# Chunk bounds on eight array tiles at once, some transposes by DMA, and a written-out order, in a chunk-selecting attention with a phase mixer

## The chip, the cores and the metric

The kernel runs on one core of a Trainium2 chip. The metric is the device time of one execution, in microseconds (us). TensorE (PE) multiplies; VectorE (DVE) and ScalarE (ACT) move results out of PSUM, the memory that PE writes; GpSimd (POOL) converts types and masks; SyncE (SP) issues every DMA, in order. Each engine works through its own queue in order.

## The reference

```python
# q, k, v: (4 batches, 8 heads, 768 positions, 64), fp32; chunks of 32 positions, so 24 chunks
ub = np.sum(np.maximum(q * k_min, q * k_max), axis=-1)     # bound of each query on each chunk (k_min, k_max: per chunk)
ub = np.where(causal, ub, -1e9)
top_chunks = np.argsort(ub, axis=-1)[..., -6:]             # six chunks for each query
scores = np.where(sel & causal_pos, q @ k.T / 8, -1e9)
x = softmax(scores) @ v                                     # heads side by side: (4, 768, 512)
theta = x @ w_theta
zr, zi = x * np.cos(theta), x * np.sin(theta)
y = w_tok_r @ zr + w_tok_i @ zi                             # over the 768 positions
u = x + y
out = u + np.maximum(u @ w_ch, 0)
```

## The kernel before

A batch has two groups of four heads. For a group, `keys` reduces k to the chunks' maxima and minima (three DVE steps for each) and writes them, with signs, to `bnd`. `queries` turns q on PE (fp32, into `psq`) and splits it by sign into two `ubq` tiles of two heads each, 64 rows of the 128 for a head. `choice` multiplies `bnd` and `ubq` in fp32 on PE (tile `psub`, L517), copies the result to `ubm`, turns it on PE (`psut`, L532), adds the causal mask (`ubs`, L537), finds the sixth largest of 24 with DVE's MAX8 (`top`, L547) and compares (L558); the result goes into `qe`, next to q, and a DMA transpose gives `qext`. It does all this in two parts, of two and of three blocks of 128 queries (`PARTS`); queries 0 to 127 need no choice. An fp32 matmul shows as two weight loads and two MATMUL records, one for each of its two passes. In L517 a matmul takes 128 rows (two heads) and 64 columns of the array, so that one part has four: two halves of the sum by two pairs of heads, the pairs on columns 0 to 63 and 64 to 127.

`attend` makes the scores of a head (`psc`, L622), the exponential (ACT, `pt`, L631), the mask on the diagonal (POOL, L642), and the product with v (`psav`, L653); DVE normalises into `x` (L669). When a batch is done, `transpose16` turns x into `xT` in four pieces `c` of two heads each (six fp16 PE transposes L688 and one copy L693 for a piece), `phases` makes theta (`pst`, L708), cosine and sine (ACT, L716) and `zz` (DVE, L722), and `mixer` the token products (`psy`, in the last batch also `psz`, L749 and L751), u (DVE, L761), its transpose `uT` and the last product (`pso`, L784, `ot`, L789). In batches 1 and 2 a DMA transpose turns u (`UDMA`); in batches 0 and 3 PE does, with four transposes (L772) and a copy for each block of 128 positions. The phases and the mixer of a batch are woven into the next batch's attention; those of batch 3 stand alone at the end.

All work is handed to `Plan` as some 1450 tasks. `Plan.order` plays them through with estimated durations, keys and a table of shifts (`SHIFT`), and gives the order in which they are written; tasks that ACT or DVE can do go to one of them there. PSUM is given out as two double banks `sc` (scores, and `psz`), one `av`, and three banks `mi` for all else. 34 `fill` matmuls (L899) keep PE going at the start.

Of the kernel before, what the change touches and what calls it, by code (L numbers as in the profile page):

```python
# [9 lines left out]
FP32 = mybir.dt.float32  # L10
# [6 lines left out]
class Task:  # L17
    __slots__ = ("i", "eng", "dur", "fn", "key", "deps", "succ", "alloc", "uses", "opts", "lock", "psum",
                 "after_start", "left", "ready", "start", "end", "kind", "group", "bias")


class Plan:
# [9 lines left out]

    LAT = {"PE": 0.22, "ACT": 0.08, "DVE": 0.08, "POOL": 0.08, "SP": 2.0}

    def __init__(self, bufs, in_order, hot, boost, shift):
        self.tasks = []
        self.bufs = bufs
        self.in_order = in_order
        self.count = {}
        self.hot, self.boost = hot, boost  # L40
        self.shift, self.group = shift, None
        self.turn = {}
        self.writers, self.readers = {}, {}
        self.tag_of, self.users = {}, {}

    def add(self, eng, dur, key, fn, r=(), w=(), new=(), after=(), kind=None, lock=False):
        t = Task()
        t.i, t.eng, t.dur, t.fn, t.key, t.kind = len(self.tasks), eng, dur, fn, key, kind
        t.opts = eng if isinstance(eng, dict) else {eng: dur}
        t.lock = lock or eng == "POOL"  # L50
        t.key += self.shift.get(self.group, 0.0)
        t.group = self.group
        t.bias = self.shift.get(("dve", self.group), 0.0)
        t.deps, t.after_start, t.succ, t.alloc, t.uses = set(), set(), [], [], []
        for name, tag in new:
            self.tag_of[name] = tag
            self.turn[name] = self.count.get(tag, 0)
            self.count[tag] = self.turn[name] + 1
            self.users[name] = []
            t.alloc.append(name)  # L60
        names = [n for n, _ in new]
        t.psum = [n[0] for n in r if isinstance(n, tuple) and self.tag_of.get(n[0]) in self.hot]
        if isinstance(eng, dict) or eng in ("ACT", "DVE"):
            if t.psum:
                t.key -= self.boost
        else:
            t.psum = []
        for n in list(r) + list(w) + names:
            base = n[0] if isinstance(n, tuple) and n and n[0] in self.users else n
            if base in self.users and t not in self.users[base]:  # L70
                self.users[base].append(t)
                t.after_start.add(self.users[base][0].i)
                t.uses.append(base)
# [3 lines left out]
        for n in list(w):  # L77
            t.deps |= set(self.readers.get(n, ()))
            t.deps |= set(self.writers.get(n, ()))
            self.writers[n] = [t.i]  # L80
            self.readers[n] = []
        for n in names:
            self.writers[n] = [t.i]
        t.deps |= set(a.i for a in after)
        t.deps.discard(t.i)
        t.after_start -= t.deps | {t.i}
        self.tasks.append(t)
        return t

    def order(self):  # L90
        T = self.tasks
        for t in T:
            t.left = len(t.deps) + len(t.after_start)
            t.ready = 0.0
            t.start = None
            for d in t.deps:
                T[d].succ.append(t.i)
            for d in t.after_start:
                T[d].succ.append(t.i)
        placed = {}  # L100
        pending = {}
        freed, last = {}, {}
        for n, us in self.users.items():
            pending[n] = len(us)
        free_at = dict.fromkeys(("PE", "ACT", "DVE", "POOL", "SP"), 0.0)
        mode = [None]
        cand = {e: [] for e in free_at}
        for t in T:
            if t.left == 0:
                for e in t.opts:  # L110
                    cand[e].append(t)
        reader, port = {}, 0.0
        n_done, seq = 0, []
        now = 0.0

        def begin(t, e):
            s = max(free_at[e], now, t.ready, port if t.lock else 0.0)
            for n in t.psum:
                if n in reader and reader[n][0] != e:
                    s = max(s, reader[n][1] + 0.1)  # L120
            return s

        while n_done < len(T):
            best = None
            for e, c in cand.items():
                at = max(free_at[e], now)
                pick = None
                for t in c:
                    s = begin(t, e)
                    ok = True  # L130
                    if len(t.opts) > 1:
                        mine = s + t.opts[e] + (t.bias if e == "DVE" else 0.0)
                        for o, d in t.opts.items():
                            if o != e and begin(t, o) + d + (t.bias if o == "DVE" else 0.0) < mine:
                                ok = False
                    own = {}
                    for n in t.alloc:
                        tag = self.tag_of[n]
                        ring = placed.setdefault(tag, [])
                        m = len(ring) + own.get(tag, 0)  # L140
                        own[tag] = own.get(tag, 0) + 1
                        if tag in self.in_order and self.turn[n] != m:
                            ok = False
                            break
                        k = m - self.bufs[tag]
                        if k >= 0:
                            f = freed.get(ring[k])
                            if f is None:
                                ok = False
                                break  # L150
                            s = max(s, f)
                    if not ok:
                        continue
                    if pick is None or (max(s, at + 1e-9), t.key, t.i) < pick[0]:
                        pick = ((max(s, at + 1e-9), t.key, t.i), s, t)
                if pick and (best is None or pick[1] < best[1]):
                    best = pick + (e,)
            assert best is not None, "no task can start"
            _, s, t, _ = best
            for e in t.opts:  # L160
                cand[e].remove(t)
            t.eng = best[3]
            d = t.opts[t.eng]
            if t.kind is not None:
                if mode[0] not in (None, t.kind):
                    d += 1.3
                mode[0] = t.kind
            t.start, t.end = s, s + d
            now = s
            free_at[t.eng] = t.end  # L170
            if t.lock:
                port = t.end
            for n in t.psum:
                reader[n] = (t.eng, max(t.end, reader.get(n, (0, 0.0))[1]))
            lat = self.LAT[t.eng]
            for n in t.alloc:
                placed[self.tag_of[n]].append(n)
            for n in t.uses:
                pending[n] -= 1
                last[n] = max(last.get(n, 0.0), t.end + lat)  # L180
                if pending[n] == 0:
                    freed[n] = last[n]
            for i in t.succ:
                u = T[i]
                u.left -= 1
                same = t.eng != "SP" and list(u.opts) == [t.eng]
                u.ready = max(u.ready, t.start if t.i in u.after_start else t.end + (0.0 if same else lat))
                if u.left == 0:
                    for e in u.opts:
                        cand[e].append(u)  # L190
            seq.append(t)
            n_done += 1
        return seq

    def emit(self):
        for t in self.order():
            t.fn(t.eng) if len(t.opts) > 1 else t.fn()
# [3 lines left out]
def kernel(  # L201
# [19 lines left out]
    NM = 5  # L221
    scale = float(1.0 / np.sqrt(D))
# [17 lines left out]
    qt = P + np.arange(NM)[None, :, None] * P + np.arange(P)[:, None, None]  # L240
    cm_np = np.where(qt // CH >= np.arange(NCH)[None, None, :], 0.0, -1e9).astype(np.float32)
    cm_h = nc.inline_tensor(cm_np.reshape(P, NM * NCH), name="cmask32")
# [5 lines left out]
    cmask32 = const.tile([P, NM, NCH], FP32, name="cmask32", tag="c_cm")  # L248
# [103 lines left out]
    def act_t(n):  # L352
        return 0.19 + n / 1200.0
# [602 lines left out]
```

## Time and profile before

| | us |
|---|---|
| three runs: median (lowest to highest) | 272.23 (272.11 to 273.69) |
| the profiled execution, its own time | 271.77 |
| its span, first to last instruction | 270.0 |
| PE busy, of the span | 240.8 |
| DVE, ACT, POOL busy | 195.5, 162.0, 135.0 |

A row of a group view names line, engine, operation, tiles and shapes, then the busy time of the group, the mean of one in ns, and the idle time before them. A matmul's record lasts longer than the stretch that it keeps the array, since records overlap; the pace is read from starts.

### The profile page before, as it was taken

Reading aid. Unit: us, or ns where it says so; the run is one execution under the profiler, and the core shown is the slowest. Engines: PE = TensorE matmul, PEld = TensorE weight load, DVE = VectorE, ACT = ScalarE, POOL = GpSimd, SP = SyncE. Lnnn points to the kernel's source line nnn. Section 1 sums busy time; section 2 is a strip of 40 time slices with the busy share of each in tenths; the row PEclk is TensorE's granted clock in tenths of the full one; section 3 lists DMA queues with packets and bytes.
Section 4 is the critical chain, followed back from the end, with each engine's and each line's share of the span. In section 5 each row is a group of like instructions: output and inputs, shape, how many; then the busy total and the mean of one; then the engine's idle time right before and its main releaser. Section 6 shows DMA issues by size and latency. Waiting matters only on the chain.

```text
span 270.0 us, 5519 instructions
## 1 busy us (share of the span) xinstructions
PE 240.8 (89%) x2055; PEld 147.8 (55%) x2055; DVE 195.5 (72%) x474; ACT 162.0 (60%) x225; POOL 135.0 (50%) x188
## 2 busy tenths in 40 slices
PE   4896586978689989989999999999999999899993
PEld 1553355666434676655763477666654667434441
DVE  3959689899799594799999985997853436344453
ACT  2349647489559499271938879635687777374000
POOL 7534657668368886968642278536302555100000
PEclk9999598999869999999999999999999999999999
DMA  7897857799989789898988642337180014310123
GB/s 198 199 240 156 213 123 113 199 259 243 252 220 258 191 232 210 185 242 211 257 204 203 121 98 62 70 89 177 22 197 0 19 41 94 141 58 0 41 78 117
DMA packets 90434, 40.71 MB, mean 151 GB/s; under 512 B 83736, under 2 KB 83864, under 8 KB 89736
## 3 DMA queue, kind: packets, MB, share of 16 engines
q1 hardware_dynamic: 90408, 40.37, 61.5%
q8 instruction: 16, 0.26, 0.4%
q14 instruction: 10, 0.08, 0.1%
HBM read 26.20 MB, written 6.29 MB: 120 GB/s over the span
## 4 chain that ended last, share of the span: by engine, by line
PE 56%; DMA 16%; DVE 13%; POOL 8%; issue 3%; SPq 2%; ACT 1%; POOLq 0%; DVEq 0%; ACTq 0%
PE psy L749 8%; PE psy L751 8%; PE psc L622 8%; PE pso L784 6%; PE psub L517 5%; PE psav L653 5%; DMA w<-in_moe_w_tok_r_dram 4%; POOL pt L642 4%; DMA out_dram<-ot 4%; PE pst L708 4%; DMA q<-in_q_dram 3%; DMA w<-in_moe_w_tok_i_dram 3%; PE psq L485 2%; POOL a L809 2%; DVE h L411 2%
## 5 line engine op out<-in xcount | busy, mean ns | idle before, releaser
L631 ACT ACTIVATE pt<-psc 128x1024 f16<-128x1024 f32 (+1 forms) x96 | 83.8, 920 | 37.5 <-PE psc L622 36.4
L642 POOL TENSOR_TENSOR pt<-pt,tri 128x256 f16<-128x256 f16 x96 | 68.3, 722 | 56.8 <-ACT pt L631 55.6
L622 PE MATMUL psc<-qext,kext 88*128 88x512 f16 (+3 forms) x256 | 51.7, 317 | 2.4 <-ACT pt L631 1.6
L749 PE MATMUL psy<-zz,wtokT 128*128 128x512 f16 x120 | 45.5, 379 | 0.9 <-DVE ot L789 0.9
L751 PE MATMUL psy<-zz,wtokT 128*128 128x512 f16 x120 | 45.4, 379 | 0.0
L622 PEld LDWEIGHTS <-kext 88*128 88x128 f16 x256 | 33.8, 153 | 13.6 <-issue 4.1
L653 PE MATMUL psav<-v,pt 128*128 128x65 f16 x672 | 28.0, 194 | 2.2 <-POOL mm L429 2.1
L653 PEld LDWEIGHTS <-pt 128*128 128x128 f16 x672 | 25.3, 98 | 7.9 <-POOL pt L642 2.9
L708 PE MATMUL pst<-wtheta,xT 128*128 128x512 f16 x96 | 25.8, 410 | 1.2 <-ACT xT L693 0.5
L761 DVE TENSOR_TENSOR u<-psy,x 128x512 f16<-128x512 f32 x20 | 13.6, 688 | 16.3 <-PE psy L751 16.3
L411 DVE TENSOR_TENSOR h<-kc 96x1024 f32<-96x1024 f32 (+1 forms) x16 | 21.2, 1327 | 5.3 <-DMA kc<-in_k_dram 5.2
L789 DVE SCALAR_TENSOR_TENSOR ot<-pso,u 128x512 f32<-128x512 f32 x24 | 16.4, 688 | 11.7 <-PE pso L784 8.8
L784 PE MATMUL pso<-wch,uT 128*128 128x512 f16 x96 | 23.5, 379 | 0.6 <-DMA uT<-u 0.6
L751 PEld LDWEIGHTS <-wtokT 128*128 128x128 f16 x144 | 14.1, 98 | 15.9 <-issue 2.3
L493 ACT ACTIVATE ubq<-psq,signs 128x256 f32<-128x256 f32 (+1 forms) x30 | 14.0, 531 | 13.6 <-PE psq L485 13.5
L749 PEld LDWEIGHTS <-wtokT 128*128 128x128 f16 x144 | 14.1, 98 | 14.1
L722 DVE TENSOR_TENSOR zz<-x,cs 128x1024 f16<-128x1024 f16 x24 | 17.7, 755 | 4.8 <-ACT cs L716 4.6
L716 ACT ACTIVATE cs<-pst,pi 128x512 f16<-128x512 f32 x24 | 16.6, 693 | 7.2 <-DVE zz L722 4.9
L517 PE MATMUL psub<-ubq,bnd 128*64 128x384 f32 (+1 forms) x128 | 20.8, 463 | 0.1
L447 POOL CAST ke<-kc 96x1024 f16<-96x1024 f32 x16 | 17.4, 1097 | 6.4 <-DMA kc<-in_k_dram 6.2
L485 PE MATMUL psq<-ident,q 128*128 128x128 f32 x80 | 14.7, 310 | 5.7 <-DMA q<-in_q_dram 3.0
L475 POOL CAST qe<-q 128x768 f16<-128x768 f32 x16 | 16.1, 1010 | 6.1 <-DMA q<-in_q_dram 3.2
(69 smaller groups left out, 364.0 us busy)
## 6 DMA issues: line engine op xcount, KB each, us to landing
q<-in_q_dram SPq DMA_DIRECT2D x32, 192.0 KB, 3.6
v<-in_v_dram SPq DMA_DIRECT2D x64, 96.0 KB, 3.1
out_dram<-ot SPq DMA_DIRECT2D x24, 256.0 KB, 2.3
kc<-in_k_dram SPq DMA_DIRECT2D x7, 768.0 KB, 6.2
w<-in_moe_w_tok_r_dram SPq DMA_DIRECT2D x6, 384.0 KB, 4.7
w<-in_moe_w_tok_i_dram SPq DMA_DIRECT2D x6, 384.0 KB, 4.3
w<-in_moe_w_theta_dram SPq DMA_DIRECT2D x4, 256.0 KB, 2.7
w<-in_moe_w_ch_dram SPq DMA_DIRECT2D x4, 256.0 KB, 3.7
```

The source lines that it names most:

```text
L411: nc.vector.tensor_tensor(out=st[hn].rearrange("p (z w) d -> p z (w d)", z=2)[:, s], in0=kv[:, s, 0], in1=kv[:, s, 1], op=op)
L485: nc.tensor.transpose(t[:, o * P:(o + 1) * P], st[q32][:, n, :, :].rearrange("p x d -> p (x d)"), ident32)
L517: nc.tensor.matmul(t[64 * z:64 * z + 64, :], bnd[g][:, y, 2 * z:2 * z + 2, :].rearrange("p x c -> p (x c)"), st[u][:, y, c0:c0 + w], start ...
L622: nc.tensor.matmul(t[:, a0:a1], kx[0:KX, hj:CH * 96:NCH], qx[0:KX, q0 + a0 - o:q0 + a1 - o], start=True, stop=True)
L631: nc.scalar.activation(out=t[:, BASE[s]:BASE[s] + wa + wb], in_=st[psc][:, 0:wa + wb], func=AF.Exp, bias=0.0, scale=scale)
L642: nc.gpsimd.tensor_tensor(out=d, in0=d, in1=tri16.unsqueeze(1).broadcast_to([P, 2, P]), op=ALU.mult)
L653: nc.tensor.matmul(t[:, a, :], st[pt][:, o:o + P], v16s[g][:, x, j, :], start=(j == 0), stop=(j == a))
L708: nc.tensor.matmul(p, st[xT][:, c, t * P:(t + 1) * P], wtheta16[:, c, :], start=(c == 0), stop=(c == 3))
L722: nc.vector.tensor_tensor(out=st[zz][:, t, :, :], in1=st[cs], op=ALU.mult, in0=st[xx][:, t, :].unsqueeze(1).broadcast_to([P, 2, dm]))
L749: nc.tensor.matmul(acc(), wtokT16[:, i, 0, t * P:(t + 1) * P], st[zz][:, i, 0, :], start=(i == 0), stop=False)
L751: nc.tensor.matmul(acc(), wtokT16[:, i, 1, t * P:(t + 1) * P], st[zz][:, i, 1, :], start=False, stop=(i == NT - 1))
L784: nc.tensor.matmul(p, st[uT][:, c, :], wch16[:, c, :], start=(c == 0), stop=(c == 3))
```

## The change

Four things change.

The bounds: `choice` works on 576 queries (192 to 767) in one go, as two windows of 320 columns that start at 0 and 256 (`th`). A matmul takes one head (64 rows) and 32 columns: two heads `x` by two pairs `z` by two windows are eight positions in the array, each with two halves `y` of the sum, so 16 matmuls stand in a row. The two heads write two PSUM banks of `mi`, taken together. Then, for each bank, come one copy of 320 columns, three transposes (six in place of five for a group), one mask of 288 elements, ten MAX8, and two compares in place of one.

The transposes: pieces 0 to 2 of x are turned by DMA in batches 2 and 3 (`XDMA`), and u of blocks 0 to 3 in batch 3 (`UDMA`). x is kept with a piece's 768 x 128 values together, which changes the strides of the DVE reads of x in L722 and L761 and of the write in L669.

The order: `Plan.order`, its keys and `SHIFT` are gone; a table of numbers, `ORDER`, names the tasks in the order in which they are written, and the sign says DVE or ACT. A path for turning the token weights by DMA exists, but its set is empty.

```diff
-    UDMA = (1, 2)
+    UDMA = {(b, t) for b in (1, 2) for t in range(NT)} | {(3, t) for t in range(4)}
+    XDMA = {(b, c) for b in (2, 3) for c in range(3)}
-        for t in self.order():
-            t.fn(t.eng) if len(t.opts) > 1 else t.fn()
+        for o in self.order:
+            t = self.tasks[~o if o < 0 else o]
...
+    ORDER = (
+        0, 2, 17, 15, 1, 3, 4, 19, 5, 6, 20, 187, 8, 114, 11, 21, 22, 7, 23, 24, 13, 16, 25, 26, 27, 62, 65, 67,
...
-                for y in range(2):
-                    for z, u in enumerate(us):
-                        nc.tensor.matmul(t[64 * z:64 * z + 64, :],
-                                         bnd[g][:, y, 2 * z:2 * z + 2, :].rearrange("p x c -> p (x c)"),
-                                         st[u][:, y, c0:c0 + w], start=(y == 0), stop=(y == 1))
+            ts = [newp(n, "mi", [P, QW], FP32) for n in psub]
+            for y in range(2):
+                for th in range(2):
+                    for z, u in enumerate(us):
+                        for x in range(2):
+                            r = slice(x * D, (x + 1) * D)
+                            c = 32 * (2 * th + z)
+                            nc.tensor.matmul(ts[x][c:c + 32, :], bnd[g][r, y, 2 * z + x, :],
+                                             st[u][r, y, th * 2 * P:th * 2 * P + QW], start=(y == 0), stop=(y == 1))
...
+        if (dst[1], c) in XDMA:
+            def turn():
+                t = new(dst) if c == 0 else st[dst]
+                nc.sync.dma_start_transpose(out=t[:, c, :].rearrange("p (n t) -> p n t", t=P),
+                                            in_=st[src][:, c].rearrange("p n d -> p (n d)"))
...
-            if b in UDMA:
+            if (b, t) in UDMA:
```

Where the instructions stand now, at three places. On PE, the second group of batch 3: the end of its bounds before, where the second part stands 40 rows behind the first,

```order
L653 LDWEIGHTS pt
L653 MATMUL psav<-v_1_75,pt 128x65
L517 MATMUL psub<-ubq,bnd_77 64x384 x4
L532 MATMUL psut<-ident_58,ubm 128x128 x2
L688 LDWEIGHTS x_2149
L688 MATMUL psT<-ident_59,x_2149 128x128
```

and after:

```order
L558 LDWEIGHTS pt
L558 MATMUL psav<-v_1_75,pt 128x65
L421 MATMUL psub<-ubq,bnd_78 32x320 x16
L527 LDWEIGHTS kext_68
L527 MATMUL psc<-qext_70,kext_68 128x512
L527 LDWEIGHTS kext_68
L527 MATMUL psc<-qext_70,kext_68 128x256
```

The two parts have become one burst of 16 matmuls, a piece of the next scores stands behind it, and the turns of x that stood there are gone.

On DVE, the choice of the first group of batch 3. Before:

```order
L537 TENSOR_TENSOR ubs<-psut,cmask_62 128x192
L547 MAX top_2692<-ubs 128x8 x8
L558 TENSOR_TENSOR qe<-ubs,top_2692 128x2x4x24
L537 TENSOR_TENSOR ubs<-psut,cmask_62 128x288
L547 MAX top_2692<-ubs 128x8 x12
L558 TENSOR_TENSOR qe<-ubs,top_2692 128x3x4x24
```

After:

```order
L440 TENSOR_TENSOR ubs<-psut,cmask_62 128x288
L450 MAX top_2705<-ubs 128x8 x10
L463 TENSOR_TENSOR qe<-ubs,top_2705 128x2x3x24
L463 TENSOR_TENSOR qe<-ubs,top_2705 128x2x2x24
L450 MAX top_2705<-ubs 128x8 x10
L705 SCALAR_TENSOR_TENSOR ot<-pso,u_2306 128x512
L463 TENSOR_TENSOR qe<-ubs,top_2705 128x2x3x24
L463 TENSOR_TENSOR qe<-ubs,top_2705 128x2x2x24
```

A mask, a MAX8 row and a compare for each part have become, for each bank, a mask (the first one stands five rows ahead of this piece), a MAX8 row and two compares.

On SP, the last DMAs of the program, from the first turn of u in batch 2 on. Before:

```order
L766 DMA_TRANSPOSE uT_3159<-u_3061 128x4x128
L793 DMA out_dram<-ot 128x512
L766 DMA_TRANSPOSE uT_3325<-u_3061 128x4x128
L766 DMA_TRANSPOSE uT_3342<-u_3061 128x4x128
L766 DMA_TRANSPOSE uT_3366<-u_3061 128x4x128
L766 DMA_TRANSPOSE uT_3415<-u_3061 128x4x128
L793 DMA out_dram<-ot 128x512 x4
L766 DMA_TRANSPOSE uT_3535<-u_3061 128x4x128
L793 DMA out_dram<-ot 128x512 x7
```

After, from the fourth turn of u in batch 2 on:

```order
L682 DMA_TRANSPOSE uT_3416<-u_3105 128x4x128
L709 DMA out_dram<-ot 128x512 x2
L682 DMA_TRANSPOSE uT_3485<-u_3105 128x4x128
L682 DMA_TRANSPOSE uT_3515<-u_3105 128x4x128
L709 DMA out_dram<-ot 128x512
L591 DMA_TRANSPOSE xT_3345<-x_3203 128x6x128
L709 DMA out_dram<-ot 128x512 x3
L682 DMA_TRANSPOSE uT_3698<-u_3607 128x4x128
L682 DMA_TRANSPOSE uT_3700<-u_3607 128x4x128
L682 DMA_TRANSPOSE uT_3716<-u_3607 128x4x128
L682 DMA_TRANSPOSE uT_3724<-u_3607 128x4x128
L709 DMA out_dram<-ot 128x512 x6
```

The third turn of batch 3's x (`xT`) stands behind three writes of the output, and four turns of u (the last four `uT`) ahead of the last six writes.

## Rows read from the trace of the kernel before

**Rows 1.** The page's part 1: busy us, share of the span, instructions.

```profile
PE 240.8 (89%) x2055; PEld 147.8 (55%) x2055; DVE 195.5 (72%) x474; ACT 162.0 (60%) x225; POOL 135.0 (50%) x188
```

**Rows 2.** Five stretches: length, busy us (count) by engine, PE clock, DMA share, GB/s.

```profile
0.00:31.00 31.00, 20.37 (x125) 11.50 (x126) 23.23 (x53) 15.69 (x25) 17.26 (x31) 0.95 0.88 204
31.00:80.00 49.00, 40.53 (x384) 27.21 (x383) 41.57 (x104) 32.32 (x43) 29.54 (x41) 0.86 0.83 198
80.00:120.00 40.00, 37.14 (x363) 24.53 (x362) 30.70 (x90) 30.04 (x43) 33.69 (x44) 1.00 0.93 223
120.00:234.00 114.00, 112.34 (x1026) 70.34 (x1024) 84.57 (x206) 74.03 (x100) 54.49 (x73) 1.00 0.49 119
234.00:270.00 36.00, 30.41 (x160) 14.25 (x160) 15.42 (x25) 9.87 (x16) 0.00 (x0) 1.00 0.17 62
```

**Rows 3.** The chain that ended last, its pieces of bounds: start, us, what.

```profile
15.85 2.31 PE psub L517 x16
...
32.52 3.48 PE psub L517 x16
...
107.36 1.01 PE psub L517 x8
...
109.52 1.44 PE psub L517 x8
...
172.83 2.30 PE psub L517 x16
```

**Rows 4.** Weight loads in order of time, a part of three blocks: start, us.

```profile
189.32 0.20 PEld L517 LDWEIGHTS psub<-ubq,bnd 128*64 128x64 f32 x4
189.70 0.14 PEld L517 LDWEIGHTS psub<-ubq,bnd 128*64 128x64 f32 x2 [0.18 <-issue]
190.02 0.14 PEld L517 LDWEIGHTS psub<-ubq,bnd 128*64 128x64 f32 x2 [0.18 <-issue]
```

**Rows 5.** PE in order of time: five fp32 transposes, one pass each.

```profile
175.74 0.74 PE L532 MATMUL psut<-ident,ubm 128*128 128x128 f32 x5
```

**Rows 6.** The chain: a piece of x and a block of u turned on PE; the end.

```profile
164.76 0.34 PE psT L688 x6
...
264.24 0.40 PE psut L772 x4
...
266.40 0.69 DVE ot L789
```

**Rows 7.** DMA issues: count, KB each, median us to landing.

```profile
qext<-qe SPq DMA_TRANSPOSE x16, 4.1
uT<-u SPq DMA_TRANSPOSE x12, 2.4
```

**Rows 8.** DVE at the start, in order of time: start, us.

```profile
9.80 1.92 DVE L495 TENSOR_SCALAR ubq<-psq,signs 128x256 f32<-128x256 f32 x4
...
14.03 1.12 DVE L461 COPY kext<-pkt 64x768 f16<-64x768 f16 x2
15.19 0.36 DVE L440 TENSOR_TENSOR bnd<-psk,signs 128x192 f32<-128x192 f32 x1
18.56 0.36 DVE L537 TENSOR_TENSOR ubs<-psut,cmask 128x192 f32<-128x192 f32 x1 [3.02 <-PE psut L532]
...
22.05 1.84 DVE L411 TENSOR_TENSOR h<-kc 96x1024 f32<-96x1024 f32 x1
```

**Rows 9.** Lines L558, L537: count, shortest/median/longest ns, first and last start.

```profile
L558 DVE TENSOR_TENSOR qe<-ubs,top x14: 348/452/1309, 40.3 to 194.5; 128x192 f16<-128x192 f32 x7, 128x288 f16<-128x288 f32 x7
L537 DVE TENSOR_TENSOR ubs<-psut,cmask x16: 347/398/451, 18.6 to 192.8; 128x192 f32<-128x192 f32 x8, 128x288 f32<-128x288 f32 x8
```

**Rows 10.** Groups by form: copies of 384 columns, and the start's fills.

```profile
L525 DVE COPY ubm<-psub 128x384 f32<-128x384 f32 x6 | 3.3, 551 | 2.4 <-PE psub L517 2.4
...
L899 PE MATMUL fill<-cs 128*128 128x512 f16 x34 | 10.8, 453 | 2.0 <-DVE cs L893 2.0
```

More of the change, by code (lines that the diff above doesn't have):

```diff
@@ L17, with __init__ @@
 class Task:
-    __slots__ = ("i", "eng", "dur", "fn", "key", "deps", "succ", "alloc", "uses", "opts", "lock", "psum",
-                 "after_start", "left", "ready", "start", "end", "kind", "group", "bias")
+    __slots__ = ("i", "eng", "fn", "opts", "deps")
 class Plan:
[L33 to L44, printed above, removed]
+    def __init__(self, bufs, in_order, hot, order):
+        self.tasks, self.order, self.group = [], order, None
+        self.bufs, self.count, self.tag_of, self.turn = bufs, {}, {}, {}
+        self.users, self.writers, self.readers = {}, {}, {}
@@ L46, in add @@
     def add(self, eng, dur, key, fn, r=(), w=(), new=(), after=(), kind=None, lock=False):
         t = Task()
-        t.i, t.eng, t.dur, t.fn, t.key, t.kind = len(self.tasks), eng, dur, fn, key, kind
+        t.i, t.eng, t.fn = len(self.tasks), eng, fn
         t.opts = eng if isinstance(eng, dict) else {eng: dur}
[L50 to L54, printed above, removed]
+        t.deps = set(a.i for a in after)
@@ L55, in add @@
         for name, tag in new:
-            self.tag_of[name] = tag
-            self.turn[name] = self.count.get(tag, 0)
+            self.tag_of[name], self.turn[name] = tag, self.count.get(tag, 0)
             self.count[tag] = self.turn[name] + 1
[L59 to L67, printed above, removed]
@@ L84, in add @@
-        t.deps |= set(a.i for a in after)
         t.deps.discard(t.i)
-        t.after_start -= t.deps | {t.i}
         self.tasks.append(t)
         return t
[L90 to L193, printed above, removed]
@@ L195, in emit @@
-    def emit(self):
-        for t in self.order():
-            t.fn(t.eng) if len(t.opts) > 1 else t.fn()
+    def emit(self):
+        done = set()
+        for o in self.order:
+            t = self.tasks[~o if o < 0 else o]
+            assert t.deps <= done, (t.i, t.deps - done)
+            done.add(t.i)
+            if len(t.opts) > 1:
+                t.fn("DVE" if o < 0 else "ACT")
+            else:
+                t.fn()
+        assert len(done) == len(self.tasks) == len(self.order)
@@ L221 @@
     NM = 5
+    Q0 = 6 * CH
+    QN = S - Q0
+    QW = QN - 2 * P
     scale = float(1.0 / np.sqrt(D))
@@ L496, in part @@
                                                 op0=ALU.mult, op1=ALU.max)
-                plan.add({"ACT": act_t(w) + 0.09, "DVE": dve_t(w) + 0.03}, None, key, part,
+                plan.add({"ACT": act_t(w - off) + 0.09, "DVE": dve_t(w - off) + 0.03}, None, key, part,
                          r=[(psq, 0), "signs"], w=[(ub, i, y)])
@@ L561, in choice @@
-            plan.add("DVE", dve_t(nb * 96) + 0.05, key, sel, r=[(ubs, i), (top8, i), "qe0"],
-                     w=[("qe", "sel", i)] if not lead else [(sl, i)], new=[(sl, "a16")] if lead and i == 0 else [], lock=True)
+                    full = qe[:, x::2, 1:, D:KX]
+                for a0, o in ((0, full[:, :, 0:3]), (3, full[:, :, 3:5])):
+                    n = 3 if a0 == 0 else 2
+                    nc.vector.tensor_tensor(
+                        out=o, in0=st[ubs][:, x, a0:6:2].rearrange("p a z c -> p z a c"),
+                        in1=st[top8][:, x, a0:6:2, :, 5:6].rearrange("p a z c -> p z a c").broadcast_to([P, 2, n, NCH]),
+                        op=ALU.is_lt)
@@ L563, in choice @@
+            plan.add("DVE", dve_t(240) + 0.3, key + 0.01 * x, sel, r=[(ubs, x), (top8, x), "qe0"] + [(sl, "new")] * (lead * x),
+                     w=[("qe", "sel", x)] if not lead else [(sl, x)] + [(sl, "new")] * (1 - x),
+                     new=[(sl, "a16")] if lead and x == 0 else [], lock=True)
         last = plan.tasks[-1]
```

198 lines of the change are left out of this document (75 added, 123 removed), and 78 rows, old and new, of tables (ORDER, SHIFT).

## Prediction

> **What bounds the kernel now.** I read the page's first part, then five stretches, then the chain of waits, then single lines. PE is busy 89% of the span, the next engine 72% [rows 1]; such an average hides stages, so the stretches decide [rows 2]. From 80 to 234 us PE is busy 149.5 of 154 us at the full clock (1.00, which is 2.4 GHz), DVE and ACT 75% and 68% of it: there a PE instruction that goes is time that goes. In the last 36 us PE is idle 5.6 us, 3.6 of them from the last sum on DVE at 266.40 to the end [rows 2, 6]. The first 80 us are another matter: PE is idle 10.6 us and then 8.5 us, the granted clock is 0.95 and 0.86 in the mean (part of the time at 1.2 GHz), 10.8 us of its busy time are fills [rows 10], and DVE is busy 65 of 80 us. There work saved on PE is worth something only where it lies on the chain.
>
> **The bounds.** A burst of both parts takes 2.30 to 2.31 us on the chain, the parts apart 1.01 and 1.44 us, 2.45 together; at the halved clock one took 3.48 [rows 3]. Inside a part of 384 columns the weight loads come two at a time, the two in 0.14 us, and such a pair comes each 0.32 us [rows 4]: eight passes in four steps, 4 x 0.32 = 1.28, and 0.16 us of edges make the 1.44. A pass alone runs at the pace of the fp32 transposes: five of 128 columns in 0.74 us, with 0.27 for the last one's own latency about 0.11 each [rows 5], so 384 columns need 0.33. Two passes thus share a step. They can't be the two passes of one matmul, which need the same 64 columns of the array with other weights; they are the two column halves side by side. That is the one thing that the trace shows of tiles: two at once cost what one does, 2.0 to 2.1 cycles a column.
>
> After, a burst has 16 matmuls or 32 passes of 320 columns; a step is 0.32 x 320/384 = 0.267 us. If eight run at once there are four steps: 1.07, with the same edges 1.23 us. If four do, eight steps: 2.30. If only two do, 16 steps: 4.43. No row shows more than two, nor halves by rows; I take eight, because rows 4 and 5 show the pace of a tile to be its own, and since each bank has its own 64 rows and each window its own 32 columns no tile shares array cells with another. At 1.23 us a contiguous burst gives back 1.07 and a split one 1.22. After 80 us there are five groups, two contiguous and three split: 2 x 1.07 + 3 x 1.22 = 5.8 us. Against that, six `psut` transposes for five, 0.11 us x 5 = 0.55 us.
>
> The loads of rows 4 all take 128 rows, those under the running passes included, and the steps follow without a gap: loads are hidden before, and I take them as hidden after. The Trainium skill, page "TensorE: Matmul & The Clock Gate", section "Part 3: Packing small matmuls — row/col tiling", speaks against it: a weight load overlaps running matmuls only when it goes to another row group, and the second pass of each tile goes to the same rows. By that rule a burst would be longer by its loads, which is rival (4) below; the trace as it stands doesn't agree.
>
> A new wait comes with it: the burst takes two of the three `mi` banks together. Until a copy has freed one (0.55 us for 384 columns [rows 10]), only one bank serves the other PE work. In the piece shown, 0.4 us or more of scores, which use `sc`, stand behind the burst. The price is 0 where such work stands there and at most the copy, 0.55, where none does; I take 0.1 x 5 = 0.5 us, and 0 to 2.7 for the range. DVE pays for four compares in place of two: by the medians some 0.35 to 0.45 us each [rows 9], so 0.6 us more a group, hidden in the stretches where DVE is at three quarters.
>
> **The turns by DMA.** A piece of x costs PE 0.34 us [rows 6]; six pieces go: 2.0 us, all after 160 us where PE bounds. Their six copies leave ACT and DVE, worth nothing there. A block of u costs 0.40 us at the end of the chain [rows 6], which holds the latency of four transposes; at the pace of a piece of x it would be 0.23. Four blocks go: 0.9 to 1.6, I take 1.0. The new DMAs land after about 2.4 us for 128 KB of u and, between that and 4.1 us for 384 KB [rows 7], an estimated 2.8 for a piece of x. DMA share is 0.49 and 0.17 in those stretches [rows 2], so they meet little. What can show is their place in SP's queue: the third turn of batch 3's x stands behind three output writes, and SP waits there for `ot`; behind the turn wait the other three writes of batch 2. PE has two heads' products, three blocks of the last product and the last piece of x to do until it needs the turned piece, SP's wait and some 2.8 us of landing run beside; which ends later no row tells: 0 to 1.5 us, taken as 0. In the tail the token products of one to two blocks stand between a u turn and its use; without that cover each would cost 2.4 us less 0.4.
>
> **The start.** `bnd` of the first group is ready at 15.55 [rows 8]. Between the first reductions DVE did four splits of q (1.92) and two copies (1.12); now two splits stand ahead of it and no copy, so up to 2 us go. The first burst is on the chain, 2.31 to 1.23: 1.1 us. Then comes a loss: from the burst's end to the last compare it was 18.16 to 22.05, with one part's copy hidden behind the other's matmuls; now a copy, three transposes, and two rounds of mask, MAX8 and two compares follow in a row, some 1.4 us more. Net 1.7, with 0 to 3 for the range. The second and third burst lie where DVE sets the pace: 0.
>
> **The order.** Each engine's order is new throughout. Idle time and the half clock before 80 us are the most that a better one could give back (some 20 us and 8), but the same DVE and DMA work (DMA share 0.83 to 0.93 until 120 us [rows 2]) stands there. No row tells its sign: taken as 0, with 6 either way. The new strides of x keep runs of 128 values; 0.
>
> **The sum.** 5.8 - 0.55 - 0.5 + 2.0 + 1.0 + 1.7 = 9.5 us off the profiled execution's 271.8: 262.3. The median of the three runs is 0.46 above that execution; I forecast 262.5. About 1% is what a measurement of this kernel can tell from no change.
>
> **Rivals.** (1) *Four at a time.* If columns of one row half can't all run at once, or the two row halves can't, a burst is 2.30, and the bounds gain only the split ones' edges, 0.45. The rest stays (2.0 + 1.0 - 1.05), the start gives 0.6: about 3 us, 268.8. For it: no row shows four. Against: the pairs show no loss at all. (2) *Two at a time, slower.* The two passes of a matmul are neighbours in the queue; if a pass that waits for its own tile holds up those behind it, only neighbours overlap. A burst is then 4.43 us: 2 x 2.13 + 3 x 1.98 = 10.2 us lost after 80 us, another 4.3 for the first three, less 2.5 gained elsewhere: 284. It decides from two tiles a step on. The same page of the Trainium skill, same section, has the rule: matmuls start and end strictly in program order. Rows 4 and 5 bear it out badly: with it a part of four matmuls would need five steps, since each one's second pass would start with the next one's first, and it takes four. (3) *The order takes it back.* The bounds and turns gain what they should, and a stall of 6 to 9 us in the first 120 us, where DMA and DVE are near full, eats it: 268 to 271.
>
> (4) *The loads show.* If the second passes' loads wait for the first passes, three of a burst's four steps grow by 0.14 us [rows 4]: 0.42 a burst, 2.1 in the five, 264.4. Against: the gapless steps of today.
>
> **Chances.** Forecast 0.63, (4) 0.05, (1) 0.13, (3) 0.10, (2) 0.09. The range runs from 254.5 (forecast less 6 of order and 2 of the start) to 269.5, which takes in (1). Faster by over 1%: forecast, (4), two thirds of (1) and half of (3), 0.81. Within 1%: 0.09. Slower: 0.10.
>
> **What would show it.** Right: the burst as 32 records in about 1.3 us on PE with eight starts within a few hundredths, PE busy near 230 us, the stretch that ends with the last score shorter by about 7 us, the turn of x landing in 2.5 to 3 us with PE not waiting for it. Wrong: starts of the burst in pairs or fours 0.27 us apart; idle time of PE on copies of `psub`; PE idle in the first 80 us longer than 19 us; or PE work down as said and the span not, which would mean that order or DMA, not PE, set the time after 80 us.

## The result, and the profile after

The changed kernel took 263.33 us in the middle of four runs (259.97 to 267.88), the kernel before 272.96 beside it (272.11 to 275.13); the ratio is 0.9542, 95% interval [0.9427, 0.9657]. A ratio here compares only the runs within 1.5% of a kernel's fastest, so it is not that of the two middles. On two further chips its middle was 270.22 us (six runs, 259.79 to 273.75) and 265.15 us (six, ratio 0.9609 [0.9527, 0.969]), so over all sixteen runs it is 265.3 us, and its runs lie 14 us apart where those of the kernel before (269.9 to 276.2) lie 6 apart. The profiled execution, 265.08 us with a span of 263.3, is one of the slower ones, at a mean granted clock of 0.948 where the two fastest of the four had 0.965 and 0.980.

The page's first part and the five stretches, beside [rows 1, 2] (the last stretch now ends at 263.3):

```profile
PE 236.0 (90%) x2139; PEld 145.8 (55%) x2139; DVE 185.3 (70%) x470; ACT 167.0 (63%) x236; POOL 132.5 (50%) x188
```

```profile
0.00:31.00 31.00, 21.16 (x147) 11.93 (x147) 23.43 (x54) 14.85 (x23) 16.35 (x33) 1.00 0.88 190
31.00:80.00 49.00, 41.80 (x465) 29.81 (x466) 39.90 (x125) 35.63 (x52) 35.16 (x45) 0.76 0.95 210
80.00:120.00 40.00, 38.63 (x356) 25.32 (x354) 34.62 (x59) 30.52 (x44) 27.05 (x37) 1.00 0.99 229
120.00:234.00 114.00, 111.24 (x1076) 68.81 (x1073) 76.60 (x218) 82.40 (x114) 53.90 (x75) 1.00 0.61 132
234.00:263.30 29.30, 23.17 (x105) 9.95 (x103) 10.78 (x17) 3.63 (x7) 0.00 (x0) 0.94 0.24 72
```

PE has less to do although it has more instructions, and from 80 to 234 us it is as full as before. Two stretches are new: from 31 to 80 us the granted clock is 0.76 in the mean for 0.86, and in the tail PE idles 6.1 of 29.3 us, for 5.6 of 36.0.

The bounds, in the chain of waits (start, us, what), beside [rows 3], and one burst on PE's matmul and weight-load sides in order of time, beside [rows 4]:

```profile
37.21 2.44 PE psub L421 x31
...
120.84 1.40 PE psub L421 x32
135.05 1.30 PE psub L421 x30
166.60 1.24 PE psub L421 x32
```

```profile
166.53 0.72 PEld L421 LDWEIGHTS psub<-ubq,bnd 64*32 64x32 f32 x32
...
166.53 1.31 PE L421 MATMUL psub<-ubq,bnd 64*32 64x320 f32 x32
```

All 32 passes are over in 1.24 us, for 2.30 or 1.01 + 1.44 before; the record of each pass alone is 0.43 us. In the records eight start within 0.05 us of each other; there are four such steps, the second 0.293 us behind the first, the others 0.269 apart (0.53 at 1.2 GHz, the 2.44 at 37 us).

The turns by DMA (issues: count, KB each, median us to landing), beside [rows 7]:

```profile
qext<-qe SPq DMA_TRANSPOSE x16, 3.9
uT<-u SPq DMA_TRANSPOSE x16, 2.4
xT<-x SPq DMA_TRANSPOSE x6, 2.9
```

DVE at the start, in order of time, beside [rows 8]: `bnd` comes at 15.26 us, for 15.19 before, with less ahead of it; the row above it shows DVE waiting for PE's transposes of q.

```profile
13.57 0.60 DVE L398 TENSOR_SCALAR ubq<-psq,signs 128x384 f32<-128x384 f32 x1
14.51 0.62 DVE L398 TENSOR_SCALAR ubq<-psq,signs 128x384 f32<-128x384 f32 x1 [0.34 <-PE psq L388]
15.26 0.36 DVE L342 TENSOR_TENSOR bnd<-psk,signs 128x192 f32<-128x192 f32 x1
```

DVE's groups by form (count, busy us, mean ns, idle us before them), beside [rows 9, 10]: a compare is 0.28 to 0.35 us, a copy 0.49 for 0.55.

```profile
L440 DVE TENSOR_TENSOR ubs<-psut,cmask 128x288 f32<-128x288 f32 x16 | 7.2, 450 | 4.1 <-PE psut L435 3.1 <-DMA cmask<-cmask 0.7
L463 DVE TENSOR_TENSOR qe<-ubs,top 128x144 f16<-128x144 f32 x14 | 4.9, 352 | 0.0
L463 DVE TENSOR_TENSOR qe<-ubs,top 128x96 f16<-128x96 f32 x14 | 4.0, 283 | 0.0
L429 DVE COPY ubm<-psub 128x320 f32<-128x320 f32 x6 | 2.9, 486 | 4.1 <-PE psub L421 4.0
```

And a stall that was not there, in the chain of the tail and as DVE's and PE's rows (idle time before them, and what ended it, in brackets):

```profile
248.84 0.85 SPq L682
249.79 3.79 DMA out_dram<-ot
253.70 0.57 DVE ot L705
254.31 0.69 DVE u L676
255.04 0.63 PE psut L688 x8
```

```profile
248.00 0.69 DVE L705 SCALAR_TENSOR_TENSOR ot<-pso,u 128x512 f32<-128x512 f32 x1 [0.17 <-PE pso L700]
...
253.70 0.69 DVE L705 SCALAR_TENSOR_TENSOR ot<-pso,u 128x512 f32<-128x512 f32 x1 [4.14 <-DMA out_dram<-ot]
...
255.04 0.62 PE L688 MATMUL psut<-ident,u 128*128 128x128 f16 x8 [1.90 <-DVE u L676]
```

The third block of output waits for a free buffer of the ring of two, until the first block has been written. The first block is ready at 248.69 us, but SP is busy with the last turn of u (L682) until 249.69, and the write starts at 249.79. Behind the third block on DVE stands the last sum, and behind that PE.

**Where the time went.** Both kernels do the same steps, so the starts of the same few PE instructions cut the span into five pieces: to the first output product of batch 0 (A), to that of batch 1 (B), to the last value product (C), to the first token product of batch 3 (D), to the end (E). All in us, one trace each, those of the experiments below with them (c0 and c1 are the changed kernel again):

```
            first score   A       B      C      D      E     span
before         23.30   110.90  46.83  73.91   9.53  28.84  270.00
after          24.80   111.07  43.87  69.81   7.50  31.04  263.30
c0             24.41   117.16  43.82  69.94   7.52  29.92  268.36
c1             23.77   112.81  42.93  70.00   7.56  29.99  263.28
e1 burst x2    25.04   115.29  45.07  71.41   7.82  31.00  270.60
e2 turns PE    24.15   108.06  43.41  73.71   8.24  28.90  262.31
e3 both        25.12   114.93  45.08  75.42   8.29  28.88  272.61
e4 u on PE     24.31   114.07  42.93  69.33   7.56  29.03  262.92
e5 three ot    23.79   109.94  42.31  69.70   7.02  28.36  257.32
e6 gap fills   22.99   108.47  43.46  70.02   7.52  28.94  258.41
e7 by tile     24.89   111.09  43.40  69.76   7.84  31.03  263.14
e8 ot, fills   23.17   110.86  43.13  69.33   6.22  28.51  258.04
e9 k first     22.47   116.39  42.93  70.07   7.72  29.74  266.86
e10 all        21.78   108.07  43.33  69.50   6.45  28.49  255.84
```

B, C and D together are 9.1 us shorter than before, A is as long, and E is 2.2 longer. That is not yet where the gain lies, since the new order moved work from the later pieces into A. One of the two lines of token products on PE, up to the end of A, before and after:

```profile
L751 PE MATMUL psy<-zz,wtokT 128*128 128x512 f16 x18 | 6.8, 379 | 0.0
```

```profile
L666 PE MATMUL psy<-zz,wtokT 128*128 128x512 f16 x30 | 11.3, 378 | 0.0
```

The other line has as many, so A now holds 24 more token products, which are 5.2 us at 0.215 us from start to start, and 14 more matmuls of scores, but four groups of bounds where it held five. So a part of the 9.1 us is work that now stands in A, which is as long as before in spite of it. The rows from `after` on have one order, but for what each experiment changes, and can be compared piece by piece.

### The profile page after: what moved, and what is told of

Read it like the earlier page. It is cut to its first block, busy times and chain, and to the rows that moved or that the text cites. A ratio compares the mean times of both kernels' runs of the same rounds, so it can differ in the third digit from the quotient of the medians.

```text
span 263.3 us, 5707 instructions
## 1 busy us (share of the span) xinstructions
PE 236.0 (90%) x2139; PEld 145.8 (55%) x2139; DVE 185.3 (70%) x470; ACT 167.0 (63%) x236; POOL 132.5 (50%) x188
## 4 chain that ended last, share of the span: by engine, by line
PE 66%; DMA 10%; DVE 9%; ACT 7%; SPq 4%; issue 2%; POOL 1%; DVEq 0%; POOLq 0%; ACTq 0%
PE psc L527 12%; PE psy L664 9%; PE psy L666 9%; PE pst L622 8%; PE pso L700 7%; PE psav L558 7%; DMA out_dram<-ot 5%; PE psub L421 3%; DMA kc<-in_k_dram 3%; PE psq L388 2%; ACT pt L536 2%; SPq L283 2%; ACT kext L363 2%; PE psz L664 2%; PE psz L666 2%; DVE top L450 2%
## 5 line engine op out<-in xcount | busy, mean ns | idle before, releaser
L536 ACT ACTIVATE pt<-psc 128x1024 f16<-128x1024 f32 (+1 forms) x96 | 85.3, 917 | 29.1 <-PE psc L527 19.8
L547 POOL TENSOR_TENSOR pt<-pt,tri 128x256 f16<-128x256 f16 x96 | 66.3, 704 | 50.7 <-ACT pt L536 50.2
L527 PE MATMUL psc<-qext,kext 88*128 88x512 f16 (+3 forms) x256 | 56.0, 328 | 2.6 <-ACT pt L536 2.0
L527 PEld LDWEIGHTS <-kext 88*128 88x128 f16 x256 | 34.7, 154 | 18.1 <-issue 6.9
L558 PEld LDWEIGHTS <-pt 128*128 128x128 f16 x672 | 30.3, 101 | 8.3 <-DVE x L574 1.4
L558 PE MATMUL psav<-v,pt 128*128 128x65 f16 x672 | 33.3, 198 | 1.4 <-DVE x L574 0.7
L700 PE MATMUL pso<-wch,uT 128*128 128x512 f16 x96 | 25.7, 398 | 1.7 <-ACT ubq L396 1.1
L622 PE MATMUL pst<-wtheta,xT 128*128 128x512 f16 x96 | 23.8, 379 | 2.1 <-DVE ot L705 1.6
L396 ACT ACTIVATE ubq<-psq,signs 128x384 f32<-128x384 f32 (+1 forms) x40 | 19.1, 512 | 7.5 <-PE psq L388 6.1
L388 PE MATMUL psq<-ident,q 128*128 128x128 f32 x80 | 16.0, 320 | 5.2 <-DMA q<-in_q_dram 4.3
L574 DVE TENSOR_TENSOR x<-psav,rec 128x384 f16<-128x384 f32 x32 | 17.7, 553 | 0.8
```

The source lines that it names most:

```text
L388: nc.tensor.transpose(t[:, o * P:(o + 1) * P], st[q32][:, n, :, :].rearrange("p x d -> p (x d)"), ident32)
L396: nc.scalar.activation(out=o, in_=i_, func=AF.Relu, bias=0.0, scale=signs[:, y:y + 1])
L527: nc.tensor.matmul(t[:, a0:a1], kx[0:KX, hj:CH * 96:NCH], qx[0:KX, q0 + a0 - o:q0 + a1 - o], start=True, stop=True)
L536: nc.scalar.activation(out=t[:, BASE[s]:BASE[s] + wa + wb], in_=st[psc][:, 0:wa + wb], func=AF.Exp, bias=0.0, scale=scale)
L547: nc.gpsimd.tensor_tensor(out=d, in0=d, in1=tri16.unsqueeze(1).broadcast_to([P, 2, P]), op=ALU.mult)
L558: nc.tensor.matmul(t[:, a, :], st[pt][:, o:o + P], v16s[g][:, x, j, :], start=(j == 0), stop=(j == a))
```

## The experiments

Theory A: the time went because PE has less to do where PE bounds. Theory B: the written-out order of the instructions brought it. Theory C: what varies from run to run lies in piece A, and is half-clock time.

**c0, the changed kernel again** (beside e1 to e3).

> The changed kernel itself, as the yardstick of the three beside it. Both theories: within 1% of its first four runs' middle, that is 260 to 266 us, with a spread of some 8 us between runs, which follows the granted clock of the first 80 us (first four: 258.2 us span at 0.980, 266.1 at 0.953).

270.22 us (259.79 to 273.75): the spread is larger than expected, the middle 4 us outside. The mean granted clock of a run does not order the times either: 0.965 for 259.79 us, 0.960 for 268.79. Its trace differs from the first one by 6.1 us in piece A and by no more than 0.13 in B, C and D.

**e1, every burst twice.**

```diff
-            for y in range(2):
+            for y in (0, 1, 0, 1):
                 for th in range(2):
```

> Every burst of bounds is run twice over, with the same result: 32 matmuls, 64 passes, for 16 and 32; nothing else moves. Theory A (the time went because PE has less to do where PE bounds): a burst is 2.3 us again, about what both parts took before; five groups after 80 us cost 5 x 1.07 = 5.4 us, the three at the start up to 1.1 each, so 5.4 to 7 us over the changed kernel. Theory B (the new order of the instructions gives the time, the work was beside it): under 1.5 us over the changed kernel.

274.03 us (12 runs), ratio to before 0.9917 [0.9865, 0.9969]; 3.8 over c0 and 8.7 over the middle of the sixteen, 8 to 10 by the ratios (0.9542 and 0.9609 for the changed kernel, on other chips), where 5.4 to 7 were expected. A burst takes 2.31 us on the chain. B, C and D, in which four of the eight groups lie (the other four are in A), are 3.1 us longer than in the first trace (3.0 than in c0, 3.8 than in c1); four times 1.07 would be 4.3. Theory A, with some 0.8 us a burst there, and not theory B. The rest of the whole runs' difference has to lie in A, with the other four bursts; one trace, 115.29 us where the changed kernel has 111.07 to 117.16, can't show it.

**e2, the ten turns on PE again**, and **e3, both undone.** The tasks of the list are renumbered; each transpose stands where its DMA stood, or as soon after as a `mi` bank comes free, which moves the output product of block 1 of batch 2 behind some other tasks.

```diff
-    UDMA = {(b, t) for b in (1, 2) for t in range(NT)} | {(3, t) for t in range(4)}
-    XDMA = {(b, c) for b in (2, 3) for c in range(3)}
+    UDMA = {(b, t) for b in (1, 2) for t in range(NT)}
+    XDMA = set()
```

> The six pieces of x and the four blocks of u are turned on PE again, with their copies on ACT and DVE, each placed where its DMA stood or as soon after as a bank of mi is free; the bounds stay eight at once. Theory A: 6 x 0.34 = 2.0 and 1.0 us for u, so 3 us over the changed kernel, less up to 1.5 if DVE no longer waits for the output writes that stand behind the turns of u. Theory B: under 1 us either way.

> Bursts twice over and the ten turns on PE: PE then has about the work of the kernel before, in the changed kernel's order. Theory A: 8 to 10 us over the changed kernel, so within 1% of the kernel before (0.99 to 1.01 of it). Theory B: 2 us over the changed kernel at most, 0.96 to 0.97 of the kernel before. In between, the share that is missing is the order's.

e2: 267.0 us (six runs), ratio 0.9738 [0.9673, 0.9803], below c0's middle. The middles can't tell a turn's worth, since piece A varies by more; the pieces behind it can. From A's end on, e2 takes 2.0 us more than the first trace, e3 2.4 more than e1: the size expected of theory A. But the parts are not those of the prediction: B, C and D grow by 4.2 (e2) and 4.5 (e3 against e1), E shrinks by 2.1 both times. e3: 273.79 us, ratio 0.9979 [0.993, 1.0027], as theory A expected. With about the work of before, the new order as a whole is worth nothing that can be measured; theory B falls. e3 differs from e2 in the doubled bursts alone, and is 6.6 us slower by the ratios, on one chip. By the ratios, then, the bursts are worth 6.6 us or more of the gain, and the turns 1.7 (e3 over e1) to 5 (e2 over the changed kernel).

**e4, only the four blocks of u on PE**, the second half of the first line above.

> Only the four blocks of u of the last batch are turned on PE again; the pieces of x stay with DMA. The prediction's step: 1.0 us more than the changed kernel. What the trace with both kinds of turns on PE suggests: from the start of the last batch's products (at 232 us) to the end 2.1 us less than the changed kernel's 31.0, since the first output writes then go out before the wait for them falls due.

265.87 us, ratio 0.9725 [0.9655, 0.9795]. Piece E is 29.03 us, as expected from the trace (2.0 less than the first one, 0.9 to 1.0 less than c0 and c1), not the prediction's 1.0 more. The whole runs don't show that gain: by the ratio e4 is slower than the changed kernel (0.9542 and 0.9609). Its piece A is 114 us, though the edit changes nothing on PE in A. Against e2, which differs in the pieces of x alone, B, C and D are 5.5 us shorter. There the forms of the x transposes on PE (count, busy us, mean ns, idle us before them) are, in e2:

```profile
L602 PE MATMUL psT<-ident,x 128*128 128x128 f16 x48 | 3.8, 219 | 0.6 <-DVE ot L705 0.3 <-DVE u L676 0.2
```

and in the same stretch of the changed kernel:

```profile
L602 PE MATMUL psT<-ident,x 128*128 128x128 f16 x12 | 1.0, 220 | 0.0
```

So 2.8 us of records for six pieces. Records overlap; by the starts a piece keeps PE 0.33 us, as one of the six in e2 shows:

```profile
220.37 0.50 PE L602 MATMUL psT<-ident,x 128*128 128x128 f16 x6
220.70 0.62 PE L527 MATMUL psc<-qext,kext 88*128 88x512 f16 x3
```

Six are 2.0 us. The other 2.2 us (4.2 against the first trace) to 3.5 us (5.5 against e4) are waits, before the transposes and where tasks had to be moved; PE's idle time alone is 1.1 to 1.7 us more in B to D. How much of that rest any order with the transposes on PE would have is open.

**e5, a third output buffer.**

```diff
-        "cs": ([P, 2, dm], FP16, 2), "ot": ([P, dm], FP32, 2),
+        "cs": ([P, 2, dm], FP16, 2), "ot": ([P, dm], FP32, 3),
```

> The ring of output tiles gets a third buffer, all else as changed. If DVE's wait for a free output tile is what holds up PE late (1.61 us before 228.8 and 1.90 us before 255.0): the first goes, the second shrinks by some 1.3 us, so about 2.9 us less than the changed kernel from 216 us to the end. If the turns' or the writes' own landing is what is late: no change there.

260.84 us, ratio 0.9554 [0.9498, 0.9609], not clear of the changed kernel's (0.9542, 0.9609); the gain shows in the pieces. From the first output product of batch 2 to the end it takes 44.2 us, for 47.4 in the first trace: 3.2 less, and 2.1 less than c0 and c1. The third block of output no longer waits for a write; the fourth does, for less:

```profile
248.16 0.69 DVE L705 SCALAR_TENSOR_TENSOR ot<-pso,u 128x512 f32<-128x512 f32 x1 [1.90 <-PE pso L700]
249.03 0.69 DVE L676 TENSOR_TENSOR u<-psy,x 128x512 f16<-128x512 f32 x1 [0.17 <-PE psy L666]
250.89 0.69 DVE L705 SCALAR_TENSOR_TENSOR ot<-pso,u 128x512 f32<-128x512 f32 x1 [1.17 <-DMA out_dram<-ot]
```

The ring is the cause of the late stall. Of E's 31 us one more goes to the clock: in the three traces with 31.0 it falls to 1.2 GHz some 7 us before the end, behind the stall, while PE still works; in c0 and c1, with the same stall and no fall, E is 29.9 to 30.0.

**e6, fills in the idle time before q.**

```diff
-            nc.tensor.matmul(t[:, 0:512], st[fz][:, 0, 0:P], st[fz][:, 0, :], start=True, stop=True)
+            for _ in range(10 if i == 8 else 1):
+                nc.tensor.matmul(t[:, 0:512], st[fz][:, 0, 0:P], st[fz][:, 0, :], start=True, stop=True)
```

> Nine more empty fills on PE in the idle time before the first q has landed (5.0 to 9.7 us), where nothing waits for PE; all else as changed. If the half-clock time in the first 90 us (27 and 34 us in two traces of the changed kernel, 17 before) comes of the idle start: the first fall comes later, half-clock time is 17 us or less, and the runs' middle falls from 268 to some 261 us with less spread. If it comes of what PE does between 20 and 50 us: no change, middle of 265 to 271 us.

261.45 us (259.35 to 266.21), ratio 0.9583, beside e5's 0.9554; no run of the changed kernel stands on that chip. Its trace has 17.1 us at 1.2 GHz before 111 us and the first fall at 34.7 us, as expected; but e5, without the fills, had 6.8, and e10, with them, 23.9. One trace each doesn't settle that the fills do it.

**e7, the burst queued tile by tile.**

```diff
-            for y in range(2):
-                for th in range(2):
-                    for z, u in enumerate(us):
-                        for x in range(2):
+            for th in range(2):
+                for z, u in enumerate(us):
+                    for x in range(2):
+                        for y in range(2):
```

> The 16 matmuls of a burst are queued tile by tile, the two of a tile (four passes to one place of the array) behind each other, in place of one matmul of each of eight tiles in turn. If a waiting pass lets the passes behind it go ahead, a burst stays at 1.24 us. If passes start strictly in the order of the queue, tile after tile has to wait for three of the four passes of the one before: 25 steps of 0.27, some 6.7 us a burst. If the queue looks a few passes ahead: between, with starts in groups of two or four tiles.

PE's row of the burst at 166 us:

```profile
166.08 1.35 PE L421 MATMUL psub<-ubq,bnd 64*32 64x320 f32 x32
```

One run, 264.91 us. The burst takes 1.35 us for 1.31: the eight tiles now start 0.013 us after each other, within 0.1 us, and the steps are 0.269 as before. Four passes to one place in a row don't hold up those behind them, so passes start out of the order of the queue.

**c1, the changed kernel a third time, and e8, e9, e10** on one chip. e8 is e5 and e6 together; e10 is all three. e9 has one line of the list of tasks changed, task 1 (the second half of the first `kc`) ahead of task 2 (`ident32`) on SP's queue, as before:

```diff
-        0, 2, 17, 15, 1, 3, 4, 19,
+        0, 1, 2, 17, 15, 3, 4, 19,
```

> The changed kernel once more, beside the three that follow. Theory C (the spread of its times, 260 to 274 us so far, is made of half-clock time in the first 110 us): the first block of output product starts between 108 and 117 us; what lies behind it is as in two earlier traces within 0.3 us (43.8 us to the second batch's, 69.8 from there to the last value product, 7.5 to the last batch's mix), and 29 to 31 us of tail. Rival: later stages vary as well.

> Third output buffer and nine fills in the idle time before q, together. Theory C, and the wait for a free output tile as cause of the late stalls: the tail from the last batch's mix 28.4 us in place of 29 to 31, the middle of the runs 2 to 6 us under the changed kernel on the same chip, half-clock time before 110 us at 17 us or less. If the fills had no part in their run's lower times: half-clock time of 17 to 34 us as without them, and 1 to 3 us under the changed kernel.

> On SP's queue the second half of the first k goes out ahead of the fp32 identity again, as in the kernel before; nothing else moves. If that place is why the first q lands 2 us later than before (PE's first q transpose at 9.4 to 9.9 us in seven traces, 7.75 before): it starts at 7.5 to 8 us and the first score 1 to 2 us earlier, at 23 us. If not: 9.4 to 9.9 and 24 to 25 us.

> Third output buffer, nine fills, and the second half of the first k ahead of the identity. If each does what the runs before suggest: 256 to 260 us in the middle, 0.94 to 0.955 of the kernel before, with a smaller spread than the changed kernel. If the place of k decides nothing: as the run with output buffer and fills, within 1%.

c1: 265.15 us. C, D and E as expected, B 0.9 shorter, since the burst at 136 us doesn't wait in c1 as it does in the first trace and c0 (see "The wait for `mi`" below): theory C holds for where the spread lies, with one us in B.

e8: 261.19 us (259.51 to 262.68), 4.0 under c1, E 28.5 us, 17.1 us at half clock: as expected. By the ratios it is 1.5 us (0.9554 for 0.9609, the intervals overlap), so what the fills add to the buffer stays open. The spread is 3 us for c1's 9.

e9: 263.96 us, ratio 0.9624, as c1. PE's first transposes of q, in the changed kernel and in e9:

```profile
9.73 1.30 PE L388 MATMUL psq<-ident,q 128*128 128x128 f32 x5 [4.25 <-DMA q<-in_q_dram]
```

```profile
7.87 1.30 PE L388 MATMUL psq<-ident,q 128*128 128x128 f32 x5 [2.39 <-DMA q<-in_q_dram]
```

1.9 us sooner, and the first score at 22.47 us for 24.80 (23.77 in c1, on the same chip). So the place of one transfer of 64 KB cost the start 1.3 to 2.3 us; why q lands later behind it, no row shows. Its piece A is long all the same, 116.4 us, and DVE's and POOL's rows show one stall in it:

```profile
96.03 3.44 DVE L313 TENSOR_TENSOR h<-kc 96x1024 f32<-96x1024 f32 x1
99.50 4.45 DVE L318 TENSOR_TENSOR h<-h 96x512 f32<-96x512 f32 x1
```

```profile
96.80 0.82 POOL L725 CAST a<-w 128x768 f16<-128x768 f32 x1
97.57 0.83 POOL L500 CAST v<-v 128x768 f16<-128x768 f32 x1
98.36 1.64 POOL L547 TENSOR_TENSOR pt<-pt,tri 128x256 f16<-128x256 f16 x1
99.95 0.82 POOL L725 CAST a<-w 128x768 f16<-128x768 f32 x1
100.73 0.66 POOL L547 TENSOR_TENSOR pt<-pt,tri 128x256 f16<-128x256 f16 x1
101.34 0.82 POOL L377 CAST qe<-q 128x768 f16<-128x768 f32 x1
102.12 1.28 POOL L547 TENSOR_TENSOR pt<-pt,tri 128x256 f16<-128x256 f16 x2
```

Two DVE instructions that take 1.21 and 0.69 us at 22.73 and 23.98 of the changed kernel's trace take 7.9 here, while POOL runs without a gap until 103.4 us; the second ends at 103.95, right behind POOL's first pause. PE then idles 3.9 us. The same pair took 3.9 us in the first trace of the changed kernel, 5.3 in c0 and 4.5 in c1.

e10: 258.42 us (256.94 to 263.09), ratio 0.9434 [0.9374, 0.9493], clear of c1's [0.9527, 0.969]: 6.7 us under c1 on the same chip, 15.0 under the kernel before, as expected. It beats both kernels. Its spread is no smaller than e8's.

## Why the prediction was right

The forecast was 262.5 us, and 263.33 came; over all sixteen runs 265.3, in the range as well. The main step, the burst, held. That the sum came out so close is luck: errors of both signs lay beside it.

- **The burst.** Eight at once was right: 1.24 us for 1.23, with loads hidden, so rivals (1), (2) and (4) are out. e7 shows more than was asked: a tile's second matmul stands in its queue ahead of the next tile's first, and still the eight tiles start within 0.1 us. The rule that matmuls start strictly in program order (Trainium skill, "TensorE: Matmul & The Clock Gate", "Part 3: Packing small matmuls — row/col tiling") is not what this trace shows. Nor does it hold for these passes that each engine works through its queue in order, as the text ahead of the prediction has it. The count was off: four groups, not five, lie where PE bounds, since the new order puts one ahead of 80 us. There they gave 3.1 to 3.4 us (e1, e3; 3.8 against c1), where the term was 5.8 less 1.05. Whole runs show more, 6.6 us (e3 over e2) to 8 or 10 (e1), so the four bursts in A, of which the prediction counted only the first, with 1.1 us, should be worth some 3 us or more; no trace shows it, since A varies by more.
- **The wait for `mi`.** Small, as said: PE's idle time before `psut` is 1.6 us in the whole span, 0.62 of it in the first group. The sum left out that the burst itself can wait for its second bank, as it does in the second group after 120 us:

```profile
134.10 0.72 PE L421 MATMUL psub<-ubq,bnd 64*32 64x320 f32 x2
134.31 0.69 DVE L705 SCALAR_TENSOR_TENSOR ot<-pso,u 128x512 f32<-128x512 f32 x1 [1.28 <-DMA out_dram<-ot]
135.05 1.30 PE L421 MATMUL psub<-ubq,bnd 64*32 64x320 f32 x30 [0.23 <-DVE ot L705]
```

Two passes run; the other 30 wait until DVE has taken a block of output out of the bank, and DVE had waited for a free output buffer. The burst takes 2.26 us here and 2.21 in c0, and B is 43.8 to 43.9 us; in c1, e4 and e9 it takes 1.31, and B is 42.9.
- **Pieces of x.** 2.0 us forecast, 4.2 to 5.5 measured in B to D. A piece keeps PE the 0.33 us that its row on the chain said, so the six are 2.0; what the sum left out is the waits that come with transposes on PE. The turn lands after 2.9 us, as estimated; PE waited 0.38 us for one that took 4.62.
- **Blocks of u.** 1.0 us of gain forecast, 0 to 2.1 us of loss measured in piece E, 1.0 of it the clock of three traces; whole runs don't confirm a loss (e4). The prediction asked for the cover of the turn and found it, but didn't follow the output writes, which now stand behind the turns in SP's queue and come close together; with two output buffers DVE waits for the first of them, and what stands behind DVE is late. With a third buffer the turns are worth 0.5 us (28.4 to 28.5 for 28.9 to 29.0).
- **The start.** 1.7 us forecast, −0.5 to −1.5 measured by the first score. The step looked at DVE's order alone; on SP's queue the identity had moved ahead of the second half of k, and PE got q 2 us later. With that undone the score comes 0.8 us before the kernel before's.
- **The signs that were named.** The last scores start 5.9 us sooner, for 7 said. PE is busy 236.0 us, not 230: it had 27.3 us at 1.2 GHz in this trace and 17.1 in the one of before, which no term of the sum held.
- **The order.** Taken as 0, with 6 either way: e3 gives 0.6 us, interval −0.7 to 1.9 by the ratio. Rival (3), a stall of 6 to 9 us in the first 120 us, did not come in the first trace: A is 0.2 us longer there, with the work that was moved into it. But c0's A is 6.3 us longer, with 34.1 us at 1.2 GHz and a DVE pair stretched as in e9, so some runs come near it.

## What to carry to other kernels

Small fp32 matmuls on disjoint rows and columns of the array ran side by side in both orders tried, so cut them to eight tiles before anything else; the gain is easiest to see where PE bounds. Where a transpose goes from PE to DMA, count the buffers of what is written out behind it. After a rewrite of the order compare SP's first ten issues too, and compare kernels stage by stage from the first place where two traces of one kernel agree, and only after counting that a stage holds the same work in both.

## What the runs showed of the hardware

- 32 fp32 passes of 64 rows, 32 columns of weights and 320 moving columns take 1.24 us at 2.4 GHz, in four steps of 0.269 us (2.0 cycles a column), eight tiles abreast, with the weights of a tile's next pass loaded behind the running one.
- A DVE instruction with two operands in SBUF may be held up over several POOL instructions: 3.44 and 4.45 us where 1.21 and 0.69 are usual. The Trainium skill, "SBUF — State Buffer", "SBUF: two separate sides", has the two engines share a pair of ports under an exclusive lock, held for a whole instruction; the trace agrees in kind, and DVE didn't get its turn between POOL instructions that stand close. Beside an idle POOL the two take some 1.21 and 0.69 us in every trace here. It goes the other way round too: at 51.20 us of the first trace DVE's 1.21 us instruction starts 0.03 us before a cast on POOL, keeps its time, and the cast takes 1.87 us, where the median of its line is 0.82. That this lock is the cause is read from such rows; no run took POOL's work away.
- The clock can stay low under a busy PE: at a granted 0.50 from 31 to 48 us of the changed kernel, PE was busy 14.49 of 17 us. The time at 1.2 GHz before 111 us was 23.9, 34.1 and 23.9 us in three traces of this one program. The longest goes with the longest piece A of the three (c0), but it doesn't make all of the spread: e9, with 17.1 us, has a longer piece A than c1 (116.4 for 112.8), and e10, with 23.9, a shorter one (108.1).
